# Batch 1's loads reordered, its chunks woven in sooner, and its u made by token and transposed by DMA

## The chip, the cores and the metric

The kernel runs on one core of a Trainium2 chip. The metric is device time in microseconds (us) of one execution, the median of several runs. The core has a matrix engine (TensorE, PE in the profile, with its weight loads shown as PEld), a vector engine (VectorE, DVE), an activation engine (ScalarE, ACT), a general engine (GpSimd, POOL) and a queue engine (SyncE, SP) which here only issues DMA transfers. Each engine takes its own instructions strictly in the order of the program and waits at the first one whose inputs or buffers are not ready.

## What is computed

Inputs are q, k, v of shape (4 batches, 8 heads, 768 tokens, 64), and the matrices U (768x32), V (32x768), w1 (512x2048), w2 (2048x512), all float32. First a retention with one decay per head, then a mixer over tokens of rank 32, then a two-layer network over channels:

```
state = gamma * state + k_t v_t^T            # per batch and head, gamma_h = 1 - 2^(-5-h)
y_t   = q_t state / sqrt(64)
x     = y as (batch, 768, 512)
u     = x + (x^T U V)^T
out   = u + max(u w1, 0) w2
```

## The kernel before

Matmuls take bfloat16 operands. The 768 tokens of a batch are six chunks of 128. For each chunk c of batch b the retention does these steps: `ret_in` scales k and q by powers of the decay on POOL (kd, then qd); `ret_v` casts v on ACT; `ret_T` transposes qd and kd (for batches 0 and 1 on TensorE, eight 128-column matmuls and one eviction; for batches 2 and 3 by two DMA transposes issued by SP, `ret_T_dma`); `ret_S` makes the scores, which DVE masks; `ret_O` makes the output x of the chunk from masked scores and the carried state, adds the chunk to the state's sum, and DVE masks the new state. `mix_P` multiplies all of x by U (result P_sb).

The network needs u both ways. mlp1 wants it with channels on partitions (tile uT, in two halves of 384 tokens: hf 0 and 1); mlp2's result needs u added, with tokens on partitions. There are two ways to get them:

- by channel: `mix_x` and `mix_h` (together `mix_u`) transpose three 128x128 blocks of x on TensorE and add V times P_sb with one 384-column matmul in the same PSUM bank; the eviction is a piece of uT. mlp2 then begins each 128 tokens with a Vb x P_sb matmul and adds x at its end.
- by token: `mix_n(b, j)` makes Vb x P_sb for 128 tokens (one 512-column matmul), DVE adds x (float32, kept in `res`), ACT copies it to bfloat16, and SP issues a DMA transpose of it into uT. mlp2 then needs no such matmul and adds the kept u.

Before the change, batch 0 goes by channel, batch 1 goes by channel for tokens 0 to 383 (four `mix_u`) and by token for the rest, and batches 2 and 3 go by token.

The order is written out by hand. Each batch's loop is a list of slots: n1 = 32 slots of mlp1 (one for 128 hidden channels and half the tokens: four 384-column matmuls) and then 48 slots of mlp2 (8 for each 128 tokens, two 512-column matmuls each). The `side` table says which work of the next batch is put ahead of which slot. In batches 1 to 3 the first six mlp1 slots are of hf 0 and the next six of hf 1. So batch 1's retention is woven into mlp2 of batch 0, and batch 2's and 3's into mlp1 and mlp2 of the batch before. A small planner (`Balance`) picks ACT or DVE for the evictions that are not fixed by hand.

SP's queue holds everything in the order in which the program reaches it: loads of q, k, v (256 KB each), DMA transposes, and outputs (256 KB each, after an addition on DVE). Load buffers are six deep for each of k, q, v, so a chunk's load needs the same chunk of the batch before to have been used. Batch 1's 18 loads are issued in slot 14 of batch 0's loop, held back by a tiny ACT instruction (`gate`), in the order k, q, v of chunk 0, then of chunk 1 and so on. Batch 2's chunks 0 to 2 are loaded as batch 1's chunks 2 to 4 are scaled (`EARLY`), and its chunks 3 to 5 at slots 0, 7 and 15 of batch 1's loop. Batch 3's chunks are loaded at slots 31, 36, 41, 46, 68 and 72 of batch 1's loop. The six `mix_n` of batch 2 stand at slots 62 to 67 of that loop.

Of the kernel before, what the change touches and what calls it, by code (L numbers as in the profile page):

```python
# [47 lines left out]
def kernel(  # L48
# [94 lines left out]
    def load_chunk(b, c):  # L143
        t = {}
        for src, nm in ((k, "k_n"), (q, "q_n"), (v, "v_n")):
            load_one(t, b, c, src, nm)
        staged[b, c] = (t["q_n", c], t["k_n", c], t["v_n", c])
# [38 lines left out]
    for c in range(NCK):  # L186
        staged[0, c] = (None, t0["k_n", c], t0["v_n", c])
# [74 lines left out]
    def ret_k(b, c, eng):  # L262
        q_n, k_n, v_n = staged.pop((b, c))
        kd = rmid.tile([P, H, D], bf16, tag="kd", name=f"kd_{b}_{c}", bufs=6)
        eng.tensor_tensor(kd, k_n, Gk[:, c].unsqueeze(2).to_broadcast([P, H, D]), op=ALU.mult)  # L265
        rc[b, c] = dict(kd=kd, q_n=q_n, v_n=v_n)

    def ret_q(b, c, eng):
        qd = rmid.tile([P, H, D], bf16, tag="qd", name=f"qd_{b}_{c}", bufs=4)
        eng.tensor_tensor(qd, rc[b, c]["q_n"], Gq[:, c].unsqueeze(2).to_broadcast([P, H, D]),  # L270
                          op=ALU.mult)
        rc[b, c]["qd"] = qd

    def ret_v(b, c):
        vb = rmid.tile([P, H, D], bf16, tag="vb", name=f"vb_{b}_{c}", bufs=6)
        nc.scalar.activation(vb, rc[b, c]["v_n"], AF.Copy)  # L276
# [169 lines left out]
    def mix_x(b, hf, c, bk=None):  # L446
        pieces[b, hf, c] = piece = (mm_bank("mix") if bk is None else bank(bk))[:, :HS]
        for jj in range(HS // P):
            j = hf * (HS // P) + jj
            matmul(piece[:, ts(jj, P)], xs[b][:, j, ts(c, P)], ident, P, start=(jj == 0),  # L450
                   stop=False, skip_group_check=True)

    def mix_h(b, hf, c):
        piece = pieces.pop((b, hf, c))
        matmul(piece, Ps[b][:, ts(c, P)], Vb[:, ts(hf, HS)], HS, start=False, stop=True,
               skip_group_check=True)
        if b == 0 and c % 2:
            nc.vector.tensor_copy(out=uTs[b][:, c, ts(hf, HS)], in_=piece)
        elif b == 0:
            nc.scalar.activation(uTs[b][:, c, ts(hf, HS)], piece, AF.Copy)  # L460
        else:
            evict(uTs[b][:, c, ts(hf, HS)], piece, HS)

    def mix_u(b, hf, c):
        mix_x(b, hf, c)
        mix_h(b, hf, c)
# [5 lines left out]
    def by_token(b, j):  # L472
        return b >= 2 or (b == 1 and j >= NCK // 2)
# [28 lines left out]
    def mlp2(b, j, part, of, cols=((0, DM),)):  # L502

        per = of // len(cols)
        i, part = part // per, part % per
        lo, w = cols[i]
        if part == 0:
            chp[b, j] = mm_bank()[:, :w]
            if not by_token(b, j):
                matmul(chp[b, j], Vb[:, ts(j, P)], Ps[b][:, ds(lo, w)], w, start=True, stop=False)  # L510
        ch = chp[b, j]
        for m in range(part * NM // per, (part + 1) * NM // per):
            matmul(ch, gTs[b][:, m, ts(j, P)], w2b[:, m, ds(lo, w)], w,
                   start=(by_token(b, j) and m == 0), stop=(m == NM - 1))
        if part == per - 1:
            o = res_of(b)[:, j, ds(lo, w)]
            nc.vector.tensor_tensor(o, chp.pop((b, j)),  # L517
                                    o if by_token(b, j) else xs[b][:, j, ds(lo, w)], op=ALU.add)
            bal.book("V", 0.69)
            nc.sync.dma_start(out=out[b, ts(j, P), ds(lo, w)], in_=o)  # L520
# [24 lines left out]
    def ret_side(b, at, lead, S_at, O_at, side):  # L545


        for c in range(NCK):
            put(side, max(0, at[c] - lead), lambda c=c: ret_in(b, c))
            put(side, O_at[c] - 3, lambda c=c: ret_v(b, c))  # L550
# [5 lines left out]
        if by_dma(b) and b + 1 < B:  # L556
            for c in range(NCK):
                put(side, (31, 36, 41, 46, 68, 72)[c], lambda c=c: load_chunk(b + 1, c))
        return side

    def mix_side(b, i, side):
        put(side, i + 2, lambda: mix_P(b, list(range(NCK))))
        js = [j for j in range(NCK) if by_token(b, j)]
        for n, j in enumerate(js):
            put(side, i + 5 + n, lambda j=j: mix_n(b, j))
        if b == 1:
            for c in range(NCB):
                put(side, i + 5 + len(js) + c, lambda c=c: mix_u(b, 0, c))
# [83 lines left out]
    for b in range(B):  # L652
# [5 lines left out]
        if b == 0:  # L658
# [8 lines left out]
            for c in range(NCK):  # L667
# [51 lines left out]
```

## Time and profile before

| | us |
|---|---|
| median of 3 runs | 229.07 (228.82 to 229.56) |
| profiled execution | 229.47 |
| its span | 227.7 |
| TensorE busy in it | 220.0 |
| ACT, DVE, POOL busy | 114.0, 82.3, 55.4 |

The span runs from the first instruction to the last. The granted TensorE clock was 1.000 over the whole span. The stages of the profiled execution: until about 29 us the retention and mixer of batch 0; from there batch 0's mlp1 (its mlp2 begins at 49.78), batch 1's mlp1 from 82.98, batch 2's from 133.65. In a timeline, a line gives start, time, engine, source line, operation with the tiles that it writes and reads, and how many instructions were merged. Line 115 is the helper that issues every matmul but the transposes of q and k. For a DMA, the line's time is the time of its issue on SP; the transfer lands later.

### The profile page before, as it was taken

To read this page: it belongs to the slowest core of one execution; us is meant where nothing else is said; L and a number is where in the kernel's file an instruction comes from. 1 tells how busy PE (TensorE), PEld (TensorE's weight loads), DVE (VectorE), ACT (ScalarE), POOL (GpSimd) and SP (SyncE) were. 2 spreads that over 40 slices of the span, in tenths; PEclk is the share of its full clock that TensorE was granted. 3 is DMA by queue.
4 is the path that set the end of the run, shared out by engine and by line. 5 is a ranking of instruction groups with operands and counts; after the bars stand their busy time and mean duration, and the time that the engine had idled before them with its cause. 6 is when DMAs were issued, how large, how long until landed. Compare 5 with 4: busy or idle time off the path is not lost.

```text
span 227.7 us, 4234 instructions
## 1 busy us (share of the span) xinstructions
PE 220.0 (97%) x1713; PEld 123.9 (54%) x1713; DVE 82.3 (36%) x155; ACT 114.0 (50%) x219; POOL 55.4 (24%) x63
## 2 busy tenths in 40 slices
PE   7898899999999999999999999999999999999995
PEld 2455666655566456656554445655554456654454
DVE  5587620003776440015673710035674510001221
ACT  4366777761336377767232627767134457770000
POOL 3852910026655330522035501050000000000000
DMA  7999899999999997987599959859311550001122
GB/s 177 241 242 202 112 193 206 201 208 228 219 210 270 211 243 188 196 168 100 105 236 236 250 132 217 202 101 94 94 49 46 135 146 0 0 0 49 61 79 92
DMA packets 102324, 34.95 MB, mean 154 GB/s; under 512 B 91264, under 2 KB 99328, under 8 KB 102304
## 3 DMA queue, kind: packets, MB, share of 16 engines
q1 hardware_dynamic: 97552, 30.49, 63.9%
q0 software_dynamic: 4752, 4.19, 11.7%
q8 instruction: 13, 0.21, 0.4%
q14 instruction: 7, 0.06, 0.1%
HBM read 27.46 MB, written 6.29 MB: 148 GB/s over the span
## 4 chain that ended last, share of the span: by engine, by line
PE 77%; SPq 7%; DMA 7%; DVE 3%; ACT 1%; issue 1%; POOL 1%; POOLq 0%
PE bk L115 75%; SPq L140 3%; DMA q0f<-in_q_dram 3%; SPq L296 2%; DMA qkT<-kd 2%; DVE a L373 1%; PE bk L351 1%; DMA qkT<-qd 1%; DMA uT<-x 1%; SPq L520 1%; DVE res L517 1%; DVE state L417 1%; POOL qd L306 1%; ACT q0T L312 1%; POOL kd L265 1%
## 5 line engine op out<-in xcount | busy, mean ns | idle before, releaser
L115 PE MATMUL bk<-w2b,gT 128*128 128x512 bf16 (+2 forms) x416 | 92.0, 363 | 0.0
L115 PE MATMUL bk<-uT,w1b 128*128 128x384 bf16 x512 | 84.5, 326 | 0.5 <-DMA uT<-x 0.5
L120 ACT ACTIVATE gT<-bk 128x384 bf16<-128x384 f32 x126 | 61.7, 490 | 31.8 <-PE bk L115 31.7
L115 PEld LDWEIGHTS <-w1b 128*128 128x128 bf16 x512 | 49.8, 98 | 34.3 <-issue 1.5
L115 PEld LDWEIGHTS <-gT 128*128 128x128 bf16 x416 | 37.9, 98 | 37.8 <-issue 0.8
L373 DVE TENSOR_TENSOR a<-bk,mask 128x512 bf16<-128x512 f32 x48 | 30.1, 683 | 40.4 <-PE bk L115 40.2
L265 POOL TENSOR_TENSOR kd<-k_n,Gk 128x512 bf16<-128x512 f32 x24 | 25.0, 1042 | 79.9 <-PE bk L115 47.2
L517 DVE TENSOR_TENSOR res<-bk,res 128x512 f32<-128x512 f32 (+2 forms) x17 | 10.7, 626 | 44.9 <-PE bk L115 44.9
L395 ACT ACTIVATE x<-bk 128x512 bf16<-128x512 f32 x23 | 13.7, 595 | 25.2 <-PE bk L115 25.2
L270 POOL TENSOR_TENSOR qd<-q_n,Gq 128x512 bf16<-128x512 f32 x18 | 18.7, 1042 | 10.5 <-DMA qkT<-qd 9.3
L417 DVE TENSOR_TENSOR state<-bk,bmask 128x512 bf16<-128x512 f32 x20 | 13.8, 691 | 12.5 <-PE bk L115 12.4
L276 ACT ACTIVATE vb<-v_n 128x512 bf16<-128x512 f32 x24 | 14.6, 623 | 2.2 <-DMA v_n<-in_v_dram 2.2
L115 PE MATMUL bk<-idle 128*128 128x512 bf16 x41 | 12.4, 430 | 1.2 <-DVE idle L192 1.2
L484 DVE TENSOR_TENSOR res<-bk,x 128x512 f32<-128x512 f32 x15 | 9.7, 686 | 8.0 <-PE bk L115 8.0
L486 ACT ACTIVATE x<-res 128x512 bf16<-128x512 f32 x15 | 9.3, 630 | 6.8 <-DVE res L484 6.5
L115 PEld LDWEIGHTS <-qkT 64*128 64x128 bf16 (+1 forms) x204 | 8.4, 95 | 7.4 <-issue 3.2
L124 DVE COPY qkT<-bk 128x1024 bf16<-128x1024 bf16 x3 | 2.1, 692 | 26.4 <-PE bk L351 26.4
L115 PE MATMUL bk<-vb,a 128*128 128x64 bf16 x192 | 9.5, 193 | 0.0
L115 PE MATMUL bk<-P_sb,Vb 128*128 128x512 bf16 x24 | 9.1, 380 | 0.0
L115 PE MATMUL bk<-vb,kd 128*128 128x128 bf16 x80 | 7.8, 219 | 1.2 <-DVE state L417 0.9
L120 ACT ACTIVATE qkT<-bk 128x1024 bf16<-128x1024 bf16 x3 | 3.1, 1023 | 11.3 <-PE bk L351 11.3
L115 PEld LDWEIGHTS <-a 128*128 128x128 bf16 x192 | 8.0, 98 | 0.6
(72 smaller groups left out, 104.9 us busy)
## 6 DMA issues: line engine op xcount, KB each, us to landing
k_n<-in_k_dram SPq DMA_DIRECT2D x24, 256.0 KB, 4.9
v_n<-in_v_dram SPq DMA_DIRECT2D x24, 256.0 KB, 5.1
out_dram<-res SPq DMA_DIRECT2D x23, 256.0 KB, 2.5
q_n<-in_q_dram SPq DMA_DIRECT2D x18, 256.0 KB, 5.0
w2b<-in_moe_w_ch_dram POOLq DMA_DIRECT2D x4, 512.0 KB, 17.3
q0f<-in_q_dram SPq DMA_DIRECT2D x3, 512.0 KB, 6.1
w1b<-in_moe_w_ch_dram POOLq DMA_DIRECT2D x3, 512.0 KB, 9.6
w1b<-in_moe_w_ch_dram POOLq DMA_DIRECT2D x2, 256.0 KB, 5.0
```

Of the source, the lines that this page charges most:

```text
L115: nc.tensor.matmul(o, l, r, **kw)
L120: nc.scalar.activation(o, i, AF.Relu if relu else AF.Copy)
L140: nc.sync.dma_start(out=n, in_=src[b, :, ts(c, P), :].rearrange("h p d -> p h d"))
L265: eng.tensor_tensor(kd, k_n, Gk[:, c].unsqueeze(2).to_broadcast([P, H, D]), op=ALU.mult)
L270: eng.tensor_tensor(qd, rc[b, c]["q_n"], Gq[:, c].unsqueeze(2).to_broadcast([P, H, D]), op=ALU.mult)
L276: nc.scalar.activation(vb, rc[b, c]["v_n"], AF.Copy)
L373: nc.vector.tensor_tensor(r["a"][:, e], r["s"][e].rearrange("p (n t) -> p n t", n=NP), mask4, op=ALU.mult)
L395: nc.scalar.activation(xs[b][:, c], o[0], AF.Copy)
L417: nc.vector.tensor_tensor(sb, ps.rearrange("p (n t) -> p n t", n=NP), bmask4, op=ALU.mult)
L484: nc.vector.tensor_tensor(u, h, xs[b][:, j], op=ALU.add)
L486: nc.scalar.activation(xs[b][:, j], u, AF.Copy)
L517: nc.vector.tensor_tensor(o, chp.pop((b, j)), o if by_token(b, j) else xs[b][:, j, ds(lo, w)], op=ALU.add)
```

## The change

Four things change. The loads of batch 1 get another order: k and q of chunks 0 to 2 first, each v further back. The steps of batch 1's retention stand earlier in batch 0's mlp2 (transposes from slot n1+4 rather than n1+7, four or so slots apart rather than five, the mixer at n1+32 rather than n1+38). Batch 1's u is made by token for all 768 tokens, with six DMA transposes instead of three, and `mix_u` is gone. The loads of batches 2 and 3 are split into k and q on one side and v on the other and put at other slots: for batch 2 chunks 0 and 1 as before, then k and q of chunks 2 and 3 at slots 0 and 1 of batch 1's loop, of 4 and 5 at 11 and 15, and v of chunks 2 to 5 at 19, 21, 27 and 31. For batch 3 chunks 0 and 1 stand at 31 and 36 and k and q of chunks 2 and 3 at 68 and 70 of batch 1's loop, the rest at 11 to 31 of batch 2's loop. `staged` now holds the loaded tiles by batch.

```
+    def load_parts(b, c, parts):
+        for x in parts:
+            load_one(staged.setdefault(b, {}), b, c, SRC[x], x + "_n")
+    def load_first():
+        for what in ("k0", "q0", "k1", "q1", "k2", "q2", "v0", "k3", "q3", "v1", "k4", "q4", "v2",
+                     "k5", "q5", "v3", "v4", "v5"):
+            load_parts(1, int(what[1]), what[0])
...
-    EARLY = (2, 3, 4)
+    EARLY = (2, 3)
...
         if b == 1 and c in EARLY:
-            load_chunk(b + 1, c - EARLY[0])
+            load_parts(b + 1, c - EARLY[0], "kqv")
...
-    def mix_u(b, hf, c):
-        mix_x(b, hf, c)
-        mix_h(b, hf, c)
...
-    def by_token(b, j):
-        return b >= 2 or (b == 1 and j >= NCK // 2)
+    def by_token(b):
+        return b >= 1
...
-            put(side, O_at[c] - 3, lambda c=c: ret_v(b, c))
+            put(side, O_at[c] - (2 if b == 1 else 3), lambda c=c: ret_v(b, c))
...
         if by_dma(b) and b + 1 < B:
-            for c in range(NCK):
-                put(side, (31, 36, 41, 46, 68, 72)[c], lambda c=c: load_chunk(b + 1, c))
+            for c, i, parts in ((0, 31, "kqv"), (1, 36, "kqv"), (2, 68, "kq"), (3, 70, "kq")):
+                put(side, i, lambda c=c, parts=parts: load_parts(b + 1, c, parts))
...
         put(side, i + 2, lambda: mix_P(b, list(range(NCK))))
-        js = [j for j in range(NCK) if by_token(b, j)]
-        for n, j in enumerate(js):
-            put(side, i + 5 + n, lambda j=j: mix_n(b, j))
-        if b == 1:
-            for c in range(NCB):
-                put(side, i + 5 + len(js) + c, lambda c=c: mix_u(b, 0, c))
+        for j in range(NCK):
+            put(side, i + (4 if b == 1 else 5) + j, lambda j=j: mix_n(b, j))
...
-            for c in range(NCK):
-                put(side, 14, lambda c=c: load_chunk(1, c))
-            at, lead, mix_at = [n1 + 7 + 5 * c for c in range(NCK)], 4, n1 + 38
-            S_at = {(0, 1): n1 + 14, (2, 3): n1 + 24, (4,): n1 + 30, (5,): n1 + 35}
-            O_at = [n1 + i for i in (19, 22, 29, 32, 35, 38)]
+            put(side, 14, load_first)
+            at, lead, mix_at = [n1 + i for i in (4, 8, 12, 18, 22, 26)], 4, n1 + 32
+            S_at = {(0, 1): n1 + 12, (2, 3): n1 + 22, (4,): n1 + 25, (5,): n1 + 29}
+            O_at = [n1 + i for i in (16, 20, 25, 28, 30, 32)]
...
         if b == 1:
-            for c, i in ((3, 0), (4, 7), (5, 15)):
-                put(side, i, lambda c=c: load_chunk(2, c))
+            for c, i in ((2, 0), (3, 1)):
+                put(side, i, lambda c=c: load_parts(2, c, "kq"))
+        if b and nxt:
+            for c, i, x in ((4, 11, "kq"), (5, 15, "kq"), (2, 19, "v"), (3, 21, "v"), (4, 27, "v"),
+                            (5, 31, "v")):
+                put(side, i, lambda c=c, x=x: load_parts(b + 1, c, x))
```

More of the change, by code (lines that the diff above doesn't have):

```diff
@@ L141, in load_one @@
         t[nm, c] = n
[L143 to L147, printed above, removed]
+    SRC = {"q": q, "k": k, "v": v}
+    def load_parts(b, c, parts):
[5 more added lines that the diff above has]
+            load_parts(1, int(what[1]), what[0])
     Uf = wts.tile([P, NCK, RK], fp32)
@@ L185 @@
             load_one(t0, 0, int(what[1]), k if what[0] == "k" else v, what[0] + "_n")
-    for c in range(NCK):
-        staged[0, c] = (None, t0["k_n", c], t0["v_n", c])
+    staged[0] = t0
     nc.sync.dma_start(out=Uf, in_=moe_U.rearrange("(j p) r -> p j r", p=P))
@@ L262, in ret_k @@
     def ret_k(b, c, eng):
-        q_n, k_n, v_n = staged.pop((b, c))
+        k_n = staged[b]["k_n", c]
         kd = rmid.tile([P, H, D], bf16, tag="kd", name=f"kd_{b}_{c}", bufs=6)
         eng.tensor_tensor(kd, k_n, Gk[:, c].unsqueeze(2).to_broadcast([P, H, D]), op=ALU.mult)
-        rc[b, c] = dict(kd=kd, q_n=q_n, v_n=v_n)
+        rc[b, c] = dict(kd=kd)
     def ret_q(b, c, eng):
         qd = rmid.tile([P, H, D], bf16, tag="qd", name=f"qd_{b}_{c}", bufs=4)
-        eng.tensor_tensor(qd, rc[b, c]["q_n"], Gq[:, c].unsqueeze(2).to_broadcast([P, H, D]),
+        eng.tensor_tensor(qd, staged[b]["q_n", c], Gq[:, c].unsqueeze(2).to_broadcast([P, H, D]),
                           op=ALU.mult)
@@ L275, in ret_v @@
         vb = rmid.tile([P, H, D], bf16, tag="vb", name=f"vb_{b}_{c}", bufs=6)
-        nc.scalar.activation(vb, rc[b, c]["v_n"], AF.Copy)
+        nc.scalar.activation(vb, staged[b]["v_n", c], AF.Copy)
         bal.book("A", 0.63)
         rc[b, c]["vb"] = vb
-    EARLY = (2, 3, 4)
+    EARLY = (2, 3)
     def ret_in(b, c):
@@ L444, with mix_x @@
     pieces = {}
-    def mix_x(b, hf, c, bk=None):
-        pieces[b, hf, c] = piece = (mm_bank("mix") if bk is None else bank(bk))[:, :HS]
+    def mix_x(b, hf, c, bk):
+        pieces[b, hf, c] = piece = bank(bk)[:, :HS]
         for jj in range(HS // P):
@@ L456, in mix_h @@
                skip_group_check=True)
-        if b == 0 and c % 2:
+        if c % 2:
             nc.vector.tensor_copy(out=uTs[b][:, c, ts(hf, HS)], in_=piece)
-        elif b == 0:
+        else:
             nc.scalar.activation(uTs[b][:, c, ts(hf, HS)], piece, AF.Copy)
-        else:
-            evict(uTs[b][:, c, ts(hf, HS)], piece, HS)
-    def mix_u(b, hf, c):
-        mix_x(b, hf, c)
-        mix_h(b, hf, c)
     res = {}
-    def by_token(b, j):
-        return b >= 2 or (b == 1 and j >= NCK // 2)
+    def by_token(b):
+        return b >= 1
     def res_of(b):
@@ L508, in mlp2 @@
             chp[b, j] = mm_bank()[:, :w]
-            if not by_token(b, j):
+            if not by_token(b):
                 matmul(chp[b, j], Vb[:, ts(j, P)], Ps[b][:, ds(lo, w)], w, start=True, stop=False)
@@ L513, in mlp2 @@
             matmul(ch, gTs[b][:, m, ts(j, P)], w2b[:, m, ds(lo, w)], w,
-                   start=(by_token(b, j) and m == 0), stop=(m == NM - 1))
+                   start=(by_token(b) and m == 0), stop=(m == NM - 1))
         if part == per - 1:
@@ L517, in mlp2 @@
             nc.vector.tensor_tensor(o, chp.pop((b, j)),
-                                    o if by_token(b, j) else xs[b][:, j, ds(lo, w)], op=ALU.add)
+                                    o if by_token(b) else xs[b][:, j, ds(lo, w)], op=ALU.add)
             bal.book("V", 0.69)
@@ L666 @@
                 put(side, 4 + s, lambda s=s: load_w2(s))
-            for c in range(NCK):
-                put(side, 14, lambda c=c: load_chunk(1, c))
-            at, lead, mix_at = [n1 + 7 + 5 * c for c in range(NCK)], 4, n1 + 38
-            S_at = {(0, 1): n1 + 14, (2, 3): n1 + 24, (4,): n1 + 30, (5,): n1 + 35}
-            O_at = [n1 + i for i in (19, 22, 29, 32, 35, 38)]
+            put(side, 14, load_first)
+            at, lead, mix_at = [n1 + i for i in (4, 8, 12, 18, 22, 26)], 4, n1 + 32
+            S_at = {(0, 1): n1 + 12, (2, 3): n1 + 22, (4,): n1 + 25, (5,): n1 + 29}
+            O_at = [n1 + i for i in (16, 20, 25, 28, 30, 32)]
         if b:
```

## The prediction

> **What bounds the kernel now.** I read the page's busy times first, then the waits, then the timelines of TensorE and of SP around the hand-overs from one batch to the next, then POOL's.
>
> ```profile
> PE 220.0 (97%) x1713; PEld 123.9 (54%) x1713; DVE 82.3 (36%) x155; ACT 114.0 (50%) x219; POOL 55.4 (24%) x63
> ```
>
> ```profile
> PE bk L115 <- DMA uT<-x: 0.5, 1, 0.5
> ```
>
> The first is the page's line, the second one of the waits (us, times, longest). TensorE is busy 220.0 of 227.7 us; about 4 us of the rest lie before 30 us and 3 us in the last 5 us, neither touched by the change. So time comes only from TensorE work taken out, or from its few stalls. The stretch that the change rebuilds, in TensorE's timeline (start, time, engine, line, operation):
>
> ```profile
> 53.02 0.39 PE L351 MATMUL bk<-ident,qd 128*128 128x128 bf16 x4
> 53.24 0.39 PE L351 MATMUL bk<-ident,kd 128*128 128x128 bf16 x4
> ...
> 78.86 0.38 PE L115 MATMUL bk<-P_sb,Vb 128*128 128x512 bf16 x1
> 79.07 0.60 PE L115 MATMUL bk<-w2b,gT 128*128 128x512 bf16 x2
> ...
> 81.56 0.33 PE L115 MATMUL bk<-ident,x 128*128 128x128 bf16 x3
> 81.73 0.33 PE L115 MATMUL bk<-Vb,P_sb 128*128 128x384 bf16 x1
> 81.89 0.59 PE L115 MATMUL bk<-w2b,gT 128*128 128x512 bf16 x2
> ```
>
> Starts tell the price, since matmuls overlap: a slot of mlp2 (two 512-column matmuls) is 0.43 us, one 512-column matmul 0.215 (78.86 to 79.07), a piece of u in mix_u 0.33 (81.56 to 81.89). SP's timeline at the hand-over to batch 3, where nothing else is on the queue, and POOL's at batch 1's first chunk:
>
> ```profile
> 175.81 2.56 SPq L488 DMA_TRANSPOSE uT<-x  x2
> 178.46 0.53 SPq L520 DMA_DIRECT2D out_dram<-res  x1
> 179.08 5.17 SPq L488 DMA_TRANSPOSE uT<-x  x4
> ```
>
> ```profile
> 50.05 1.04 POOL L265 TENSOR_TENSOR kd<-k_n,Gk 128x512 bf16<-128x512 f32 x1 [20.55 <-PE bk L115]
> 51.06 1.03 POOL L270 TENSOR_TENSOR qd<-q_n,Gq 128x512 bf16<-128x512 f32 x1
> ```
>
> Six transposes are 1.30 us apart on SP, an output among them adds 0.62, and the last lands at 185.46: 9.65 us from the first issue to the last landing (one alone: 2.5). POOL's first kd of batch 1 starts 0.16 us after its k landed (49.89 in the trace), whatever the row names.
>
> **What leaves and enters TensorE's queue.** In batch 0's loop four mix_u go (4 x 0.33 = -1.32) and three mix_n come (3 x 0.215 = +0.65): -0.67. In batch 1's loop mlp2 of tokens 0 to 2 no longer begins with a Vb x P_sb matmul: 3 x 0.215 = -0.65. Both lie on the path. DVE gets three additions (0.69 each) and ACT three copies (0.63), less four evictions of u (ACT 0.48, DVE 0.56). mix_n comes every 0.65 us and DVE starts one every 0.60 back to back, so they hide beside mlp2 and cost only as links of the chain below.
>
> **The old stall at batch 1's first mlp1.** TensorE's starts at 83.15, 83.39, 83.80 stand 0.33 us further apart than the 0.16 of such matmuls: the evictions of the last mix_u. They are gone: -0.33.
>
> **The sooner weave.** The stage starts at 49.78 as before. The first transposes of batch 1 move from slot n1+7 to n1+4: 49.78 + 0.215 + 4 x 0.431 = 51.72. They need qd, which POOL ended at 52.09; k0 and q0 stay first in the load queue, so this row holds: wait to about 52.2, +0.48, and all that follows on TensorE's queue moves with it. Its cover before was three slots (1.3 us). For the later chunks I put the new order of loads on the old landings (49.89, 50.61, 51.70, 52.66, 53.84, 55.00, then about 1.2 apart, the 18th at 69.37): k1 and q1 come third and fourth, so qd of chunk 1 ends at 54.1 and is needed at 54.4; for chunks 2 to 5 the slack is 0.2 to 1.3 us. Each v lands before its cast; the cast of v0 ends within 0.2 us of O(1,0), the state of chunk 2 within 0.2 us of O(1,3), that of chunk 4 within 0.1 of O(1,5), as DVE works nearly back to back there (masks, 0.60 apart). Also the scores of chunk 3 are written to the bank that O(1,2) takes three slots later, not five: its third mask ends 0.2 us ahead. Those waits are worth 0 to 0.44; the same working on the old order gives 0.17 at a place where the trace shows none, so I take 0.12, near the low end. Together +0.60 (bounds 0.3 and 0.95).
>
> **The transposes.** mix_n(0) stood 43 slots in; now it stands 36 in, with one residual matmul less ahead of it: 78.86 - 7 x 0.431 - 0.215 + 0.60 = 76.23. Its sum, addition and copy take 1.62 (78.86 to 80.66 was 1.80 with SP busy, x ready 80.63; 123.96 to 125.73 is 1.77; without other work 0.21 + 0.69 + 0.03 + 0.63), so the first transpose issues at 77.85. Ahead of it SP has 18 loads, chunks 0 and 1 of batch 2, and outputs 0 to 3: by its old pace (65.89 after the 18 loads, then 0.4 to 2.7 each) free at about 75.8 (the load of batch 2's first v needs the cast of batch 1's first v, done at 59.8, before SP comes to it), so it hides with 2 us to spare, and the backlog of transfers drains at about 79.8, before the first transpose would land. The third lands at 77.85 + 2 x 1.30 + 2.5 = 82.95. TensorE reaches mlp1 at 76.23 + 6.68 (six mix_n with their slots, one residual, six slots) = 82.91 and starts at 83.08: +0.17. Its second half comes six groups (3.90) later, 86.98; the sixth lands at 77.85 + 9.65 = 87.50, plus 0.13 to start (133.52 to 133.65 in the trace): 87.63, +0.65. So +0.82. The pitch decides: the rows run from 1.22 (178.37 less 177.09 and the like, issue alone) to 1.82 (127.33 to 129.15, with loads in flight), so the term runs from 0.3 to 3.9; I take 1.30, the row without loads, since the rest of batch 2's loads now queue behind the sixth.
>
> So far -0.67 - 0.33 + 0.60 + 0.82 = +0.42: the second half of mlp1 starts later than before (87.21), not sooner.
>
> **The later hand-overs.** At 132.81 TensorE waits 0.63 for the third transpose of batch 2, which sat behind SP's loads and outputs (loads issued until 125.60, first transpose 127.33 though x was ready at 125.73). Now batch 3's loads at slots 36 to 46 shrink to one chunk, and SP, counted at 1.30 a transpose and 1.1 a load from 86.4, is through at about 120.5, 5 us ahead of the first transpose. Third landing 131.4, need 132.8: -0.63. At 158.72 a 0.30 wait for qkT of batch 3 goes too: its transposes stood behind six loads (first 145.03); with four in front and the rest between, the first issues near 138.5, and the pair needed at 157.5 lands at 153.7: -0.30, even with one delay of 2.4 us such as 154.18 to 159.03. The moved loads do pass batch 2's qkT transposes on SP: with k and q of chunks 2 and 3 ahead, chunk 4's and 5's between, and v's after, the pairs land at about 98, 106 and 112 against needs of 101, 109 and 115. All hidden, 2.5 us at least; if that cover went, a late pair would cost its lateness.
>
> **Sum.** +0.42 - 0.65 - 0.63 - 0.30 = -1.16 us. The profiled execution (229.47, of which 227.7 is span) would be 228.3; it stands 0.40 above the median 229.07, so the forecast is 227.9 against the median.
>
> One rule speaks against the change: the Trainium skill's page "VectorE: DVE Perf Modes", section Rules for kernel authors, sends a 128 x 128 transpose to TensorE where the result may land in PSUM, and to the DMA otherwise. By it mix_u should have stayed, the sum being that of the moved loads alone; here the row has 1.32 us of TensorE against my 0.82 of waiting, so it is nearly a draw.
>
> **The rivals.**
> The gain is eaten at the hand-over (0.25). Pitch 1.40 (6 x 0.10) and the weave's waits at their upper bound (0.35) with one more late link of 0.05 add 1.0: 228.9. For it: every slack in the weave is under 1.3 us. Against it: the old order had slacks as small and TensorE stalled nowhere from 30 to 83 us.
> Slower (0.18). The six transposes share the DMA engines with the landing loads of batch 2 and three outputs of 256 KB and go at the 1.73 + 0.09 of the row at 127.33: 6 x 0.5 = 3 us more before the second half of mlp1, less 0.4 as only some of them meet traffic: 230.5. It decides from a pitch of about 1.49, where 6 x 0.19 eats the 1.16. For it: that row, and the landing of the transpose at 80.66, 3.5 us on. Against it: the next two there were 2.6 and 2.5, and my backlog is drained by 79.8.
> The transposes cost nothing (0.05). If 128 KB of transpose moved like half a 256 KB load (1.13 apart, so 0.57), the 0.82 would vanish: 227.1. Against it: 1.30 at 175 to 184 us with no loads about. The Trainium skill's page "Advanced Engine Details and Errata", section X-Bar Transpose (TRN2), says just this, that transposing DMAs are as fast as regular ones; this trace has twice the time per byte.
>
> **How the numbers follow.** The forecast has 0.52, its own range 227.3 to 228.4 (weave 0.3 to 0.8, pitch 1.22 to 1.35). A change under 0.3% (0.69 us) can't be told from none, so same is 228.38 to 229.76. Forecast and the free transposes are faster: 0.57; the eaten gain is same: 0.25; slower 0.18. The range 227.2 to 229.8 leaves out the slow case and most of the free one.
>
> **What would show it.** Right: no ident,x matmuls at about 81 us; a wait of about 0.5 at 51.7 for qd; TensorE waiting for uT<-x twice, near 83 and 87, 0.8 together; none at batch 2's first mlp1. Wrong: transposes of batch 1 over 1.5 apart, a first one later than 78.5, or waits for loads inside the weave.

## The result and the profile after

The changed kernel takes 231.64 us (median of 4 runs, 231.43 to 231.95) where the kernel before took 229.05 beside it (4 runs, 228.82 to 229.56). The ratio is 1.0109, with a 95% interval of 1.0090 to 1.0128: it is slower by 1.1%, where 227.9 had been forecast. The profiled execution took 231.66, its span is 229.9.

First the page's busy times, after:

```profile
PE 219.8 (96%) x1697; PEld 123.3 (54%) x1697; DVE 83.6 (36%) x157; ACT 114.7 (50%) x219; POOL 55.4 (24%) x63
```

There are 16 matmuls less: 19 are taken out (16 of `mix_u`, three of mlp2) and three put in (`mix_n`). They weigh 1.32 us by their starts, and the span grew by 2.2 us with that much less to do. So TensorE waits. (The busy time fell by only 0.2; the ends of matmuls are modelled there, so the figures below go by starts.) Its waits from 50 us on, after (us in all, times, longest; the list's other lines for TensorE lie in the first 30 us):

```profile
PE bk L115 <- DMA uT<-x: 1.3, 2, 1.1
PE bk L115 <- DVE res L516: 0.8, 1, 0.8
PE bk L115 <- DMA qkT<-kd: 0.6, 1, 0.6
PE bk L356 <- POOL qd L275: 0.4, 1, 0.4
```

Of these, only the transposes' line stood in the list of before, with 0.5. TensorE's timeline, after, at each of them (start, time, engine, line, operation, and in brackets the idle time before it with its releaser):

```profile
52.70 0.40 PE L356 MATMUL bk<-ident,qd 128*128 128x128 bf16 x4 [0.39 <-POOL qd L275]
...
83.76 4.06 PE L115 MATMUL bk<-uT,w1b 128*128 128x384 bf16 x24 [0.20 <-DMA uT<-x]
88.93 1.30 PE L115 MATMUL bk<-uT,w1b 128*128 128x384 bf16 x7 [1.11 <-DMA uT<-x]
...
110.88 0.40 PE L115 MATMUL bk<-qkT 64*128 64x128 bf16 x8 [0.61 <-DMA qkT<-kd]
...
123.09 0.38 PE L115 MATMUL bk<-state,qkT 128*128 128x128 bf16 x4 [0.81 <-DVE res L516]
```

The brackets count from the modelled end of the matmul before. Counted from start to start, less what such a matmul takes, the five waits are 0.55, 0.37, 1.27, 0.77 and 0.98 us. These are the figures used below. They are those of one execution: the first of them is 0.33, 0.15, 0.61 and none in the profiles of one, two, five and six below, where the program up to there is the same.

The stages give the balance. From the first matmul of one batch's mlp1 to the first of the next, and from the last such start to the end of the last instruction, in us:

| | before | after | difference | forecast |
|---|---|---|---|---|
| batch 0 to 1 | 54.00 | 54.35 | +0.35 | +0.10 |
| batch 1 to 2 | 50.67 | 52.08 | +1.41 | -0.96 |
| batch 2 to 3 | 49.42 | 49.08 | -0.34 | -0.30 |
| batch 3 to the end | 42.10 | 42.09 | -0.01 | 0 |
| sum | 196.19 | 197.60 | +1.41 | -1.16 |

Nearly all of the miss is in the second row: 2.37 us, which is exactly the second half's wait beyond its forecast (1.27 - 0.65 = 0.62) and the two waits that were not forecast (0.77 and 0.98). The sum differs by 1.41 us while the medians differ by 2.59. Of the rest, 0.43 lies before batch 0's mlp1, 0.35 behind the last addition of DVE, with which the sum ends, and 0.40 is what the profiled run of before stands above its median. The 0.43 is a difference between executions: the change leaves that code alone, and over the sixteen profiles of this document batch 0's mlp1 begins between 28.98 and 29.97.

The 0.35 belongs to the change. In the six profiles with 136 DMAs on SP the span ends 2.48 to 2.50 us after that addition, in the ten with 139 (three transposes more) 2.82 to 2.85. At its end SP waits for the semaphores of its last transfers one by one. That of the last output stood last in the list before; after, it is the fourth of nine, and five waits of 0.06 us follow its landing. The prediction has no term for this.

### The profile page after: what moved, and what is told of

Same layout as the page of the kernel before. It is cut to its first block, busy times and chain, and to the rows that moved or that the text cites. A ratio compares the mean times of both kernels' runs of the same rounds, so it can differ in the third digit from the quotient of the medians.

```text
span 229.9 us, 4213 instructions
## 1 busy us (share of the span) xinstructions
PE 219.8 (96%) x1697; PEld 123.3 (54%) x1697; DVE 83.6 (36%) x157; ACT 114.7 (50%) x219; POOL 55.4 (24%) x63
## 4 chain that ended last, share of the span: by engine, by line
PE 73%; DMA 13%; DVE 4%; POOL 3%; SPq 3%; ACT 2%; issue 1%; POOLq 0%; DVEq 0%
PE bk L115 71%; DMA k_n<-in_k_dram 5%; DMA q0f<-in_q_dram 3%; DMA uT<-x 2%; DMA qkT<-kd 2%; SPq L301 2%; DMA q_n<-in_q_dram 2%; POOL qd L275 1%; PE bk L356 1%; DVE res L483 1%; DVE a L378 1%; POOL kd L270 1%; SPq L140 1%; DVE res L516 1%; POOL qd L311 1%
## 5 line engine op out<-in xcount | busy, mean ns | idle before, releaser
L516 DVE TENSOR_TENSOR res<-bk,res 128x512 f32<-128x512 f32 (+2 forms) x20 | 12.7, 636 | 45.6 <-PE bk L115 45.6
L483 DVE TENSOR_TENSOR res<-bk,x 128x512 f32<-128x512 f32 x18 | 11.7, 686 | 9.9 <-PE bk L115 9.9
L485 ACT ACTIVATE x<-res 128x512 bf16<-128x512 f32 x18 | 11.1, 630 | 6.7 <-DVE res L483 6.4
L115 PE MATMUL bk<-idle 128*128 128x512 bf16 x41 | 13.2, 452 | 1.2 <-DVE idle L197 1.2
```

Of the source, the lines that this page charges most:

```text
L115: nc.tensor.matmul(o, l, r, **kw)
L483: nc.vector.tensor_tensor(u, h, xs[b][:, j], op=ALU.add)
L485: nc.scalar.activation(xs[b][:, j], u, AF.Copy)
L516: nc.vector.tensor_tensor(o, chp.pop((b, j)), o if by_token(b) else xs[b][:, j, ds(lo, w)], op=ALU.add)
```

## What the five waits are made of

SP's timeline, after, holds all but the first (for a DMA the time is that of its issue):

```profile
78.50 5.23 SPq L487 DMA_TRANSPOSE uT<-x  x4
83.86 0.49 SPq L519 DMA_DIRECT2D out_dram<-res  x1
84.47 3.03 SPq L487 DMA_TRANSPOSE uT<-x  x2
...
103.86 1.21 SPq L140 DMA_DIRECT2D v_n<-in_v_dram  x2
105.17 1.55 SPq L301 DMA_TRANSPOSE qkT<-qd  x1
106.76 1.27 SPq L301 DMA_TRANSPOSE qkT<-kd  x1
108.14 2.19 SPq L301 DMA_TRANSPOSE qkT<-qd  x1
...
114.94 0.58 SPq L140 DMA_DIRECT2D k_n<-in_k_dram  x1
115.56 0.58 SPq L140 DMA_DIRECT2D q_n<-in_q_dram  x1
116.19 1.79 SPq L140 DMA_DIRECT2D v_n<-in_v_dram  x2
```

- The first six transposes go at a pitch of 1.31, as forecast, but two things add to them. The first one comes 1.80 us after its `mix_n` rather than 1.62. And in the last row of two, which should last 2.5, SP stands still for 0.45 us between them (85.74 to 86.19). The same stop stands in the trace of before at the same place of SP's program, after its 79th instruction (waits for semaphores counted); there the next instruction was an output, for which nobody waited. Now it is the sixth transpose, for which TensorE waits. From first issue to last landing the six take 10.29 us, not 9.65.
- The pair of transposes for chunk 3 of batch 2 (105.17 and 106.76) is the one of the 0.77. I had counted it to land at 106; it landed at 110.23 and 110.83. The two loads of v ahead of it (103.86) are those of chunks 2 and 3: their slots 19 and 21 come before slot 22, where chunk 3 is transposed.
- The v of batch 2's chunk 5 is the second of the last row. It was issued at 117.18 and landed at 121.90. ACT's timeline, after, shows who stood behind it:

```profile
116.93 0.62 ACT L281 ACTIVATE vb<-v_n 128x512 bf16<-128x512 f32 x1
121.92 0.63 ACT L281 ACTIVATE vb<-v_n 128x512 bf16<-128x512 f32 x1 [4.37 <-DMA v_n<-in_v_dram]
122.46 0.58 ACT L400 ACTIVATE x<-bk 128x512 bf16<-128x512 f32 x1
```

ACT waits 4.37 us at the cast of v, and the eviction of the chunk before stands behind the cast on the same engine. TensorE's next output wants the PSUM bank (PSUM is the memory that TensorE writes to) that this eviction empties, and starts at 123.09, just after it. The list of waits names a DVE addition; by its timing that is a coincidence, and the experiments below decide it.

## The experiments

The theories that the expectations name: **S**, the stalls are separate, so that taking one away gives its time back; **Q**, SP's queue is behind over a long stretch, so that time won at one wait is lost at the next; **P**, the new places of the later loads are bad by themselves, whatever is done with u; and later **F**, SP's queue is simply full, so that no order of it wins, against an order that fits. Diffs are against the changed kernel unless another is named. All ratios are to the kernel before on the same chip, with 95% intervals.

**One: is the second half's wait worth its time?** Nine groups of batch 1's first half go first, instead of six, so that the sixth transpose has 1.95 us more (three groups).

```
-            slots = slots[:12:2] + slots[1:12:2] + slots[12:]
+            w = 18 if b == 1 else 12
+            slots = slots[:w:2] + slots[1:w:2] + slots[w:]
```

> Changed kernel, but batch 1's mlp1 does nine groups of the first half of the tokens before the second half, not six, so that the sixth transpose of u has 1.9 us more. Both theories: the 1.27 us wait near 87 us goes. Theory Q (the queue): SP's queue runs late from the six transposes on, and its later items come at the same time as before, so the next wait (qkT of batch 2's chunk 3, landing near 110.8) grows by what was won: 231.6, within 0.4 us of the changed kernel. Theory S (the stalls are separate): 1.27 less, 230.4.

231.27 us against 228.96: 1.0099 (1.0073 to 1.0124). The wait of 1.27 is gone and the whole hardly moved. TensorE's timeline of this run:

```profile
83.16 17.71 PE L115 MATMUL bk<-uT,w1b 128*128 128x384 bf16 x108 [0.19 <-DMA uT<-x]
...
108.00 0.40 PE L115 MATMUL bk<-qkT 64*128 64x128 bf16 x8
110.11 0.40 PE L115 MATMUL bk<-qkT 64*128 64x128 bf16 x8 [1.71 <-DMA qkT<-kd]
```

The time comes back 1.1 us larger at the next place: 1.87 counted from start to start, where it was 0.77. TensorE arrives earlier and SP's pair lands when it did before (26.90 us after the first matmul of batch 1's mlp1, 27.07 in the changed kernel). That is Q, for these two waits. The wait at 122 stays at 0.98.

**Two: is the wait at 122 us the load of v?** That load moves one slot up, which puts it ahead of the three loads of batch 3 that stand in slot 31.

```
-                            (5, 31, "v")):
+                            (5, 30, "v")):
```

> Changed kernel, with one load moved: v of batch 2's chunk 5 one slot sooner (30 instead of 31), so that it stands ahead of batch 3's first three loads in SP's queue and lands about 3 us sooner. If the 0.98 us wait at 121.9 is ACT standing at the cast of that v, with the eviction of chunk 4's x and so TensorE behind it, it goes: 230.7. Rival: the wait there is DVE's addition that the profile names; then nothing changes, 231.6.

230.21 against 228.96: 1.0054 (1.0035 to 1.0073). ACT's wait for v, and TensorE's for the eviction behind it, are gone:

```profile
ACT vb L281 <- DMA v_n<-in_v_dram: 1.3, 4, 0.4
```

(5.7 us, longest 4.4, in the changed kernel.) TensorE's waits at 83, 88 and 110 stay: 0.35, 1.27 and 0.77. The median fell by 1.43, more than the 0.98 of that wait; in this profile the one at 52 us is 0.15 and not 0.55, but whether that holds for the other runs is not known. So this one is a stall of its own, and its cause is the load behind ACT's cast, not the addition that the list names.

**Three: the later loads alone.** The kernel before, with only the loads of batches 2 and 3 at their new places.

```
-    EARLY = (2, 3, 4)
+    EARLY = (2, 3)
...
+            for c, i in ((2, 0), (3, 1)):
+                put(side, i, lambda c=c: load_parts(2, c, "kq"))
...
+            for c, i, x in ((4, 11, "kq"), (5, 15, "kq"), (2, 19, "v"), (3, 21, "v"), (4, 27, "v"),
+                            (5, 31, "v")):
```

> Only the new places of batch 2's and 3's loads, on the kernel before: batch 1's load order, weave and u as before. Theory Q: three transposes fewer on SP ahead of them, so the queue is 3 us less late and the new waits at 110 and 122 us do not show, while the old 0.63 at batch 2's first mlp1 and 0.30 at 158.7 go: 228.1. Rival P: the new places are bad by themselves (loads among the qkT transposes of batch 2): both waits show, 1.0 to 1.7 more less the 0.93: 229.1 to 229.9.

230.49 against 228.96: 1.0066 (1.0046 to 1.0086). Its waits for v on ACT and for ACT's eviction on TensorE:

```profile
ACT vb L280 <- DMA v_n<-in_v_dram: 6.7, 4, 5.1
PE bk L115 <- ACT x L399: 1.3, 1, 1.3
```

Here the profile names the eviction behind the cast by itself. So the place of that one v is bad without u by token and without the sooner weave (P), and costs 1.47 here; the time is above even P's 229.1 to 229.9. The wait at 110 is absent: it needs more than the moved loads (Q). The old waits of 0.63 and 0.30 are gone, as forecast.

**Four: those loads with that one v a slot up.** The kernel of three with the edit of two.

> The kernel before with only the new places of the later loads, as in the run with the loads alone, but v of batch 2's chunk 5 at slot 30 instead of 31. If that one place was the whole loss of the loads alone, its 1.47 us wait at 120 us goes and what the new places were to bring shows: 0.63 at batch 2's first mlp1 and 0.30 at 159 us: 228.1. Rival: another wait follows at once (qkT of chunks 4 and 5, pushed back by that load), 229 or more.

228.98 against 229.01: 1.0006 (0.9994 to 1.0019). The 1.47 is gone, but of the 0.93 us that should then have been left as a gain the median shows nothing. Its profiled run is 0.40 us shorter than before's from batch 0's mlp1 to the end, with four waits of 0.17 to 0.24. Of the 0.53 that are missing there, 0.40 lie between batch 0's and batch 1's mlp1 (54.40 us against 54.00), where this profile has two waits for qd at 62.8 and 67.2 us. Three has the same program up to there and 54.00 without such waits, so this is a difference between executions, and one as large as what was to be shown.

**Five: u of tokens 0 to 383 by channel again**, the rest of the change kept.

```
-    def by_token(b):
-        return b >= 1
+    def by_token(b, j):
+        return b >= 2 or (b == 1 and j >= NCK // 2)
...
+        if b == 1:
+            for c in range(NCB):
+                put(side, first + len(js) + c, lambda c=c: mix_u(b, 0, c))
```

> Changed kernel with batch 1's u as before for tokens 0 to 383 (by channel on TensorE, three transposes by DMA); new load order, weave and loads stay. Theory Q: without the three extra transposes there is no wait at 83 and 87, and the waits at 110 and 122 shrink or go since SP is 3.9 us ahead: 1.64 + 0.72 + 0.98 less, 1.32 of TensorE more: 229.6. Rival P: the waits at 110 and 122 stay, only 1.64 goes: 231.3.

230.09 against 228.96: 1.0045 (1.0021 to 1.0068). The time lies between the two forecasts, nearer to Q's. Only 0.61 at 52 us and 0.30 at 85.2 are left of the waits; those at 110 and 122 are gone, although no load has another slot. Three transposes fewer on SP (3.9 us of its time) put what stands behind them back in time: Q. The v of chunk 5 lands at 119.29, 2.6 us sooner than in the changed kernel. ACT still waits 2.61 for it, but the eviction behind has its input only 0.2 us after the cast, so nobody is held up: the place that cost 1.47 in three just does here. As it was changed, u by token lost about 1.5 us (2.59 less 1.13).

**Six: the later loads at their old places**, the rest of the change kept (`EARLY` of three whole chunks, batch 3 at slots 31, 36, 41, 46, 68, 72, batch 2's chunks 3 to 5 at 0, 7, 15).

> Changed kernel with the later loads as before (three chunks of batch 2 loaded in batch 0's loop, whole chunks at the old slots); batch 1's load order, weave and u by token stay. Three loads more stand ahead of the first transpose of u on SP: it issues 1 to 1.5 us later and the wait near 87 us grows to 2.3 to 2.8. Theory Q: the wait at 110 us shrinks by as much as TensorE is later, the one at 122 goes, the old 0.63 at 133 us comes back in part: 231 to 232. Rival (the new places are the main loss): 230 or less.

233.44 against 229.01: 1.0203 (1.0179 to 1.0227). It is worse than I expected. TensorE's timeline at batch 1's mlp1:

```profile
85.07 4.06 PE L115 MATMUL bk<-uT,w1b 128*128 128x384 bf16 x24 [2.14 <-DMA uT<-x]
90.14 3.08 PE L115 MATMUL bk<-uT,w1b 128*128 128x384 bf16 x18 [1.00 <-DMA uT<-x]
```

The first transpose is issued at 79.69, 3.6 us after its `mix_n` (76.08), since SP had to issue three more loads and two outputs from 75.71 on; 0.9 and 0.8 us of wait come at 111 and 136. So with u by token the new places are worth 1.8 us (4.43 less 2.59).

**Seven: the weave at its old slots**, the rest kept. The steps that go with it (scores, outputs, casts of v, `mix_n`) move back too; one line of the edit:

```
-            at, lead, mix_at = [n1 + i for i in (4, 8, 12, 18, 22, 26)], 4, n1 + 32
+            at, lead, mix_at = [n1 + 7 + 5 * c for c in range(NCK)], 4, n1 + 38
```

> Changed kernel with the steps of batch 1 where they were (first transposes n1+7, mixer n1+38), new load order, u by token and new later loads kept. The first transpose of u has 6.5 slots less: from mix_n(0) to mlp1 TensorE has 3.5 us of work in place of 6.7, so it waits 3 to 3.6 us at about 83 and 1 to 1.3 us at about 91, while the 0.55 at 52 goes. By theory Q the wait at 110 shrinks to 0 as TensorE is later, that at 122 too. 232.5 to 234.

233.35 against 229.11: 1.0188 (1.0161 to 1.0215). The third transpose is now 3.51 us late and the sixth 1.12 more. The waits for qkT and at the eviction shrink to 0.47 and 0.48, where by Q they were expected to vanish. So the sooner weave is what gives the six transposes their time; it is worth 1.7 us to them.

**Eight: the weave and the load order alone**, on the kernel before.

> The kernel before with only batch 1's new load order and sooner weave (u and the later loads as before). What the weave costs by itself: the wait for the first qd at 52 us, 0.2 to 0.6. The three old transposes issue sooner, so that the old stall at batch 1's first mlp1 stays 0.3 and the old 0.63 at 133 us and 0.30 at 159 us stay: 229.2 to 229.6. Rival: the compressed weave has hidden waits of its own on DVE or the banks: 230 or more.

229.28 against 229.11: 1.0004 (0.9987 to 1.0021). No difference can be told; waits of 0.18 to 0.3 come in four places. One of them is the old 0.63 at 133 us, expected to stay and now 0.23; the old 0.30 at 159 us is gone. The weave by itself is about free.

**Nine: do instruction fetches delay the pair at 110 us?** The trace has 13 packets of 16 KB on a queue of its own:

```profile
q8 instruction: 13, 0.21, 0.4%
```

They follow TensorE's instruction count, and one of them (108.2 us) falls on that pair. This kernel splits each of the idle matmuls at the start in two, which adds 82 TensorE instructions ahead and moves every later packet.

```
-            matmul(w, idle[:, :P], idle, DM, start=True, stop=True)
+            for i in range(2):
+                matmul(w[:, ts(i, DM // 2)], idle[:, :P], idle[:, ts(i, DM // 2)], DM // 2,
+                       start=True, stop=True)
```

> Changed kernel with each of the 41 idle matmuls of the start cut into two of half the width: the same array time, 82 TensorE instructions more (41 matmuls, 41 weight loads). In the traces so far a 16 KB packet of the instruction queue comes with every 250 TensorE instructions or so, and SP's issue at that moment takes 2.0 to 2.7 us instead of 0.4 to 1.3. If the packets are fetches of TensorE's instructions, each comes 82 instructions sooner, so the ones near 90.7, 108.2 and 121.9 us move to about 84, 101 and 116, and the long issues with them, and the qkT transposes near 107 land in 2.5 us. Rival: the long issues come from SP's own queue of transfers and stay with the same transfers.

232.0 in one run. The packets went from 90.7, 108.2 and 121.9 to 85.4, 103.4 and 117.4. The wait at 110 vanished: the pair, issued 0.4 us later, landed at 109.24 and 109.66, 1.0 and 1.2 us sooner: 3.62 and 2.51 us after issue instead of 5.06 and 4.07. And the fetch now at 85.4 hits the last two transposes of u:

```profile
83.40 4.06 PE L115 MATMUL bk<-uT,w1b 128*128 128x384 bf16 x24 [0.19 <-DMA uT<-x]
89.60 2.60 PE L115 MATMUL bk<-uT,w1b 128*128 128x384 bf16 x15 [2.13 <-DMA uT<-x]
```

The fifth of them took 4.9 us from issue to landing, where 2.45 is usual, and TensorE waited 2.30 instead of 1.27. The wait at 122 is 1.37 here, so the time as a whole is no shorter. TensorE came 1.03 us later to the pair (2.30 less 1.27), but even without that it would not have waited: it used the pair at 110.78, so it would have wanted it at 109.75, and could have had it at 109.71 (0.05 after the landing, as in the changed kernel). So by this estimate, from one execution each, the wait of 0.77 needs the fetch: without it the pair issued at 106.76 lands by 109.5, against a need at 110.11. The fetch takes the last of a cover that the queue's lateness had already eaten. In one, the fetch at 106.6 falls on the same pair (3.73 us instead of 2.6), and about 1.1 of its 1.87 is that.

**Ten: all the waits mended at once.** Chunk 0's transposes of q and k one slot later, nine groups first, v of chunk 5 a slot up, v of chunks 2 and 3 three and two slots later, and k and q of batch 2's chunk 2 ahead of the transposes of u, where SP stood idle for 1.6 us (the first line below stands in batch 0's loop).

```
-            for c, i in ((2, 0), (3, 1)):
-                put(side, i, lambda c=c: load_parts(2, c, "kq"))
+            put(side, n1 + 32, lambda: load_parts(2, 2, "kq"))
+            put(side, 1, lambda: load_parts(2, 3, "kq"))
```

> Changed kernel with every wait found so far taken at its cause: first transposes of batch 1 one slot later (n1+5); nine groups of the first half in batch 1's mlp1; k and q of batch 2's chunk 2 loaded in batch 0's loop, where SP stands idle for 1.6 us ahead of the first transpose of u; v of chunks 2 and 3 behind the qkT transposes of chunk 3; v of chunk 5 ahead of batch 3's loads. Theory Q: the waits at 52 (0.55), 87 (1.27), 110 (0.72) and 122 us (0.98) go, all 3.5: 228.1 at most, and since the TensorE work saved is 1.3 and the old waits at 133 and 159 are gone, at best 227. Rival: the queue is simply full from 78 to 122 us, and a wait of over 1 us shows at another place: 229 to 230.

229.24 against 229.01: 1.0009 (0.9990 to 1.0027). That is the rival's 229 to 230. All waits but one are gone, and the one that is left has grown: 1.77 for the third transpose of u, where it was 0.37. SP's timeline of this run:

```profile
76.05 0.45 SPq L140 DMA_DIRECT2D k_n<-in_k_dram  x1
76.59 1.01 SPq L140 DMA_DIRECT2D q_n<-in_q_dram  x1
77.71 6.60 SPq L487 DMA_TRANSPOSE uT<-x  x4
```

Four transposes take 6.60 us here and 5.23 in the changed kernel: the first one alone needs 2.66 (77.71 to 80.36) to issue, right behind two loads that land at 80.94 and 81.67. So the third lands too late. SP's idle 1.6 us were not free: the transfers behind it had a backlog.

**Eleven: the same loads ahead, in other places.** k and q of chunks 0 to 2 go ahead as `EARLY` of three chunks without their v, so that as many loads stand ahead of the transposes as in the changed kernel; v of chunks 0 and 1 go to slot 14 of batch 1's loop. Of ten, the slot of chunk 0's transposes, the nine groups and the places of the four v are kept.

```
-    EARLY = (2, 3)
+    EARLY = (2, 3, 4)
...
-            load_parts(b + 1, c - EARLY[0], "kqv")
+            load_parts(b + 1, c - EARLY[0], "kq")
...
-            for c, i in ((2, 0), (3, 1)):
-                put(side, i, lambda c=c: load_parts(2, c, "kq"))
+            put(side, 0, lambda: load_parts(2, 3, "kq"))
+            for c in (0, 1):
+                put(side, 14, lambda c=c: load_parts(2, c, "v"))
...
+            for c, i, x in ((4, 11, "kq"), (5, 15, "kq"), (2, 22, "v"), (3, 23, "v"), (4, 27, "v"),
+                            (5, 30, "v")):
```

> Changed kernel, mended with no more transfers ahead of the first transpose of u than it has: k and q of batch 2's chunks 0, 1, 2 are loaded in batch 0's loop in the place of k, q, v of chunks 0 and 1, whose v go behind the qkT transposes of chunk 1; v of chunks 2 and 3 behind those of chunk 3; v of chunk 5 ahead of batch 3's loads; first transposes of batch 1 at n1+5; nine groups first in batch 1's mlp1. Theory Q: the wait near 82 us stays at 0.36 (it was 1.77 with two loads more ahead), those at 87, 110 and 122 us go: 1.3 + 0.7 + 1.0 and 0.4 of the 0.55 at 52 less than the changed kernel's 231.6: 228.2 or a little less, faster than the kernel before by 0.3 to 0.7%. Rival (the queue is full at any order): a wait of 1 us or more shows between 100 and 125 us and it is 229 or more.

228.69 against 229.11: 0.9984 (0.9967 to 1.0001), inconclusive, and between the two forecasts. The wait at 83 is back at 0.35 and the one at 87 gone, but in the profile 0.61 and 0.25 stand at 53 and 55 (qd), and 0.64 and 0.67 came for transposes of q and k at 109 and 116. That profile is of an execution of 230.02, 1.3 above the median, so most runs can't have had all of these.

**Twelve: more room for each.** On eleven, the scores of batch 2 two slots later, the q and k transposes of batch 1's first three chunks one or two slots later, and two v further down.

```
+            at, lead, mix_at = [n1 + i for i in (6, 10, 14, 18, 22, 26)], 4, n1 + 32
...
+            S_at = {(0, 1): 27, (2, 3): 39, (4, 5): 49} if b == 1 else {(0, 1): 27, (2, 3): 37, (4, 5): 47}
...
+            for c, i, x in ((4, 11, "kq"), (5, 15, "kq"), (2, 22, "v"), (3, 26, "v"), (4, 30, "v"),
+                            (5, 30, "v")):
```

> The mended kernel of the run before (same count of transfers ahead of the first transpose of u) with slack where its profile still showed waits: batch 1's first transposes at n1+6 and n1+10 instead of n1+5 and n1+8 (0.86 us of waits for qd), the scores of batch 2's chunks 2 and 3 at slot 39 and of 4 and 5 at 49 instead of 37 and 47, and v of chunk 3 and 4 each behind the qkT transposes of chunk 4 and 5 (0.64 and 0.67 us of waits for qkT). TensorE's work is the same. Theory Q: those 2.2 us go and only 0.36 at 83 us stays: its profile's 230.0 less 2.2 is 227.8, its median 228.7 less 1.5 to 2.2 is 226.5 to 227.2; clearly faster than the kernel before. Rival (a full queue gives the waits back elsewhere, or the masks crowd the outputs of chunks 2 and 4): 228.5 or more.

229.13 against 229.26: 0.9993 (0.9980 to 1.0006). The q and k waits are gone; in their place TensorE waits 1.28 us up to 115.0, and the forecast of 226.5 to 227.2 is missed by two microseconds. The waits of this run name the same pattern as in two, now for chunk 3:

```profile
ACT vb L281 <- DMA v_n<-in_v_dram: 17.8, 9, 5.2
PE bk L115 <- ACT x L400: 1.1, 1, 1.1
```

**Thirteen: twelve, with the four v back where eleven had them** (slots 22, 23, 27, 30).

> The run with more slack again (batch 1's first transposes at n1+6 and n1+10, scores of batch 2 at 39 and 49), but v of batch 2's chunks 3 and 4 back at slots 23 and 27. There v of chunk 3 landed at 113.8 us and ACT stood at its cast with the eviction of x of chunk 2 behind it, 1.28 us of waiting. Theory Q with an order that fits: v of chunk 3 lands near 112, that wait goes and no other over 0.4 us comes: 227.6 to 228.2, faster than before by 0.4 to 0.7%. Theory F (SP's queue is full from 88 to 118 us, whatever the order): another wait of 0.6 us or more between 105 and 125 us, 228.8 or more.

228.05 against 229.21: 0.9953 (0.9938 to 0.9968). This is faster than the kernel before by 0.5%, as the theory of an order that fits had it (227.6 to 228.2). The page and the waits of this run:

```profile
PE 216.6 (96%) x1678; PEld 123.0 (54%) x1697; DVE 83.6 (37%) x157; ACT 115.3 (51%) x219; POOL 55.4 (25%) x63
```

```profile
PE bk L115 <- DMA uT<-x: 0.2, 1, 0.2
```

The only wait left after 50 us that is more than 0.1 beyond a matmul's own time is 0.36 at the third transpose of u (19 of the 1697 matmuls are missing in this record, and their gaps look like waits of 0.2). Theory F falls: SP has just as many DMAs to issue as in the changed kernel. From batch 0's mlp1 to the last addition its profile is 1.87 us shorter than before's; the medians differ by 1.16. Of the difference, 0.34 is the longer end of SP's waits, 0.15 a later start of batch 0's mlp1, and the rest that before's profiled run stands 0.26 above the median of the runs used here.

**Fourteen: what is u by token worth in a queue that works?** The kernel of five with the later q and k transposes of twelve and v of chunk 5 at slot 30.

> The changed kernel without its transposes: u of tokens 0 to 383 by channel, first transposes of batch 1 at n1+6 and n1+10, v of batch 2's chunk 5 at slot 30, all else as changed. No wait for qd, none for qkT or v, the old 0.30 at the last mix_u stays, the old 0.63 and 0.30 are gone: by theory Q 228.1 to 228.5. Against the run beside it this gives what u by token is worth once its waits are gone: it has 1.3 us more TensorE work, less 0.4 us of waits at batch 1's first mlp1. If the two are equal, the transposes are worth nothing even then.

229.09 against 229.21, on the chip of thirteen: 1.0000 (0.9984 to 1.0017), above the 228.1 to 228.5 that was expected. Thirteen and fourteen are 1.04 us apart, and their intervals do not touch. They differ in some places of loads too, so this is u by token with the loads ordered for it, against u by channel with only its own worst wait mended. Its profile has 0.88 at 158.8 (qkT of batch 3), but is of an execution of 230.11, 1.0 above the median, so that wait may not be in most runs.

## Why the prediction was wrong

- **The work removed** (-0.67 and -0.65): right. There are 16 matmuls fewer, and with these terms and the waits as measured the row from batch 1 to 2 adds up (-0.33 - 0.65 - 0.63 + 1.27 + 0.77 + 0.98 = +1.41), and that from 0 to 1 to 0.10.
- **The old stall of the evictions** (-0.33), **the wait for batch 2's third transpose** (-0.63) and **for batch 3's qkT** (-0.30): right, all three are gone, the last two also in the run with the loads alone. The last had luck: the pair forecast to land 3.8 us ahead of its need landed 0.4 ahead (160.51, used at 160.93), and in fourteen it was late.
- **The weave** (+0.60, bounds 0.3 to 0.95): right in this profile. The wait for qd, which the term mostly is, was 0.55 where 0.48 was written, but none to 0.61 in four others with the same program up to there, so the match in size is partly luck; `mix_n` began at 76.70, and the forecast 76.23 with the 0.43 by which this run began later is 76.66.
- **The transposes** (+0.82): mechanism right, size off. The pitch, which I had named as what decides, was 1.31 against 1.30. What I left out is a link in front (1.80 instead of 1.62, although two rows of 1.80 and 1.77 stood in my own text) and SP's stop of 0.45. The two waits were 0.37 and 1.27: +1.64. (The 1.22 named as the lower pitch is the time of an issue alone; 178.37 less 177.09 is 1.28. Only the lower bound, 0.3, rests on it.)
- **"All hidden, 2.5 us at least"**, the moved loads past batch 2's qkT transposes: this is the step that failed, twice. The pair of chunk 3, counted to land at 106 against a need at 109, landed at 110.83 against one at 110.11. "v's after" was not so: v of chunks 2 and 3 stand ahead of that pair. Counted again at the text's own 1.30 and 1.1 from 86.4, the pair lands at 106.8 without these two loads and at 109.0 with them, so that no cover was left before anything ran late. In the run, SP came to the loads 1.8 us later than counted (88.21 and not 86.4: 0.65 at the first transpose, the stop of 0.45, and a second output behind the sixth). From there to the pair it took 0.65 more than the count without the two v: these took 1.31, and the transposes right behind loads 1.35 to 1.94 each instead of 1.30, while the loads of k and q were cheaper than 1.1. Then the landing took 4.07 instead of 2.5, under a fetch. My text had a row for the last two (1.82 with loads in flight, 2.4 for one delay) and used neither there.
- **The same step for the v of chunk 5**: I gave all v one word, "after", and checked only the transposes against their needs. I had not asked what stands on ACT behind the cast of a late v. A wait of 4.37 us on an engine that is half idle reached TensorE because an eviction was queued behind it.
- **No term at all**: the 0.34 us at the end of SP's waits, by the three DMAs more.
- **The rivals.** "Slower" ended on the right side, at 230.5 against 231.64, for the wrong reason: its mechanism was a pitch of 1.8, and the pitch held. "The gain is eaten" had "one more late link" at 0.05; there were two, at 0.77 and 0.98.
- **The rule against the change**: the Trainium skill's page "VectorE: DVE Perf Modes", section Rules for kernel authors, would have kept the transposes on TensorE. For the change as made it was right: five, which does that, is 1.5 us faster. With SP's queue put in order, thirteen against fourteen says the opposite by 1.04 us, though they differ in places of loads too: where TensorE is the bound and DMA issue has room, the matmuls saved count.

The forecast gains were there to be had: thirteen has them. That it gains 1.16 us, the very number forecast, is chance, since it is spared most of the +0.60 and the +0.82 and pays the 0.34 at the end; by the terms above it would gain 1.9 (-2.58 + 0.36 + 0.34), and 0.5 to 0.7 of that is not accounted for. What was wrong was the assumption that SP's queue would give the gains for nothing.

## What to carry to other kernels

When transfers are moved, write the whole queue out in the order of the program, time it with the slow rows, not the clean ones, and check every consumer of each moved transfer, with what stands behind that consumer on its own engine: a 4 us wait on a half-idle engine becomes the bound as soon as one PSUM eviction is queued behind it. When a queue is late over a long stretch, taking away one wait moves it to the next one, so test waits together and not one by one. The waits of one profile are those of one execution: here the same code gave 0 to 0.6 us at one place, so a wait of that size needs more than one profile. A change that loses may hold a gain: the parts alone (three, four, eight) cost nothing except for the place of one load, and what lost was their meeting on one queue; edits to the order alone turned it into a gain.

## What the runs showed of the hardware

- TensorE's instructions arrive as packets of 16 KB on a DMA queue of their own, 13 in a run, about 250 TensorE instructions apart in the mean (185 to 318 after, weight loads counted; 3443 in all before, 3411 after). Adding 82 instructions at the start moved the three named above by 4.5 to 5.3 us. In the trace of before, seven SP issues fall on one between 60 and 160 us and took 1.9 to 2.7 us each, where the like take 0.4 to 1.4, and transposes right behind loads up to 1.7; transposes of the changed kernel and of nine that were under way then landed 3.4 to 5.1 us after issue, where most others take 2.4 to 2.7, or 3.0 to 4.0 if they are the first behind loads. Two of the seven rows, in SP's timeline of before:

```profile
104.43 2.37 SPq L296 DMA_TRANSPOSE qkT<-kd  x1
...
117.34 2.49 SPq L520 DMA_DIRECT2D out_dram<-res  x1
```

  The Trainium skill's page "Advanced Engine Details and Errata", section ISA Cache, gives lines of 16 KB for 256 instructions, which the spacing agrees with; the delay to other transfers is this trace's.
- SP stood still for 0.43 to 0.45 us behind the 79th instruction of its program in all sixteen profiles, whatever came next (an output before, a transpose after). Its cause is not in the trace.
- Three DMAs more made the end of the kernel 0.34 us longer, by where the last output's semaphore stands in SP's closing list of waits.
- A transpose issued right behind loads whose transfers are still in flight takes up to 2.66 us to issue instead of 1.22 to 1.30 (ten). An idle issuing queue does not mean that the transfers are drained.
- The list of waits named an addition on DVE for the wait at 122 us; the kernel with v a slot up and the one with the loads alone show that it was ACT's eviction behind a cast that waited for a load.
